# Reordering the steps of a fused attention and token-mixing kernel behind batch 0's first half

## Chip, cores and metric

The kernel runs on one core of a Trainium2 chip. The metric is device time in microseconds (us) of one execution; three runs of the kernel before gave 104.17, 104.23 and 104.53, median 104.23.

## What is computed

Per batch (8 of them) there are 8 heads of 576 rows with 64 columns, and 32 packed queries `p`. Two attentions follow each other, then a token-mixing layer whose weights depend on the data:

```python
p_packed = sm_attn(p, k, v)               # softmax(scale * p k^T) v, per head
out = sm_attn(q, p_packed, p_packed)      # softmax(scale * q p_packed^T) p_packed
x = out.transpose(0, 2, 1, 3).reshape(B, S, H * D)
wq, wk = x @ w_q, x @ w_k                 # 512 -> 64
W_tok = scale * einsum('bsd,btd->bst', wq, wk)
mixed = einsum('bst,btd->bsd', W_tok, x)
return maximum(mixed, 0) @ w_out          # 512 -> 512
```

All inputs and the output are float32; the matmuls run on bfloat16, since the loads convert on the way.

## The kernel before

The program is one written order of small steps, the string `ORDER`. A step reads `NAME.batch.part=banks@engine`: `banks` are the PSUM banks that it writes, `@V`, `@A`, `@P`, `@S` is VectorE (DVE), ScalarE (ACT), GpSimd (POOL) or SyncE (SP), and steps without a letter run on TensorE (PE), but for `LD` (loads, issued by GpSimd) and `ST`, `STF`, `STH`, `HOLD` (issued by SyncE). Each engine executes its own steps strictly in the order of the string, and waits by semaphore for the data and the buffers that a step needs. So the order decides which engine waits where. Eight PSUM banks, three to six buffers of each tile, and four buffers each for k, q and v tie the batches together.

For each batch the steps are, with the engine that does them:

- `LD.k`, `LD.v`, `LD.q`: loads; a `v` is two issues. `KT`, `QV` (DVE, line 237): transpose k and q in 32x32 blocks.
- `S1` (PE, 282), `X1` (ACT, 293), `TE` (DVE, 237): scores of the packed queries, exp, transposition. `PV` (PE, 315), `RC`, `PP` (DVE, 319 and 323): their values and division; `PP` multiplies by the tile `mask`. `PT` (DVE): transposition of the result.
- `QK` (PE, 336), `QKE` (copy out of PSUM), `QD` (POOL, 130): the packed values times `w_k` and `w_q`.
- `S2` (PE, 373), `X2` (ACT, 378), `RS`, `RR` (DVE, 394 and 399): scores of the second attention, exp, sum, reciprocal. `AM` (line 405, POOL or DVE) multiplies the exponentials by the reciprocals; `HA` is a first half of one sum on POOL.
- `AT` (PE, 414 and 419), `AE` (copy): transposition of the attention. `WKQ` (PE, 441 and 446), `WE` (copy), `GM` (PE, 467), `GE` (copy), `Y` (PE, 477), `YE` (copy with scale), `MX`, `MR` (PE, 492 and 498), `RL`, `RLF`, `RLR` (relu): the token mixing without ever forming `out`.
- `OT`, `OH` (PE, 540 and 580): four matmuls with `w_out` per 128 rows; `OE`, `OEF`, `OEH` copy them to the output tile, and the stores follow. The parts of `S2`, `X2`, `RS`, `RR`, `AM`, `AT`, `AE` are ranges of 128-row blocks: 0 is two blocks, 1 the next two, 2 the fifth, 3 all first four, 4 all five.
- `WARM.n` (PE, 619): n filling products of 128 columns on zeros, whose result nobody reads.
- `HOLD.v7`: a tiny DMA on SyncE that waits for batch 7's `v`; every store of SyncE stands behind it.

Output tiles come from six buffers, so batches 6 and 7 write into the tiles of batches 0 and 1, whose stores must have landed:

```python
copy(eng, new("o", b, [P, 4, D], fp32, bufs=NO)[:, 2 * tp:2 * tp + 2], T["ot", b, tp])   # NO = 6
```

In the order, batch b's first attention runs while batch b-1's second attention and batch b-2's output are done, so that TensorE always has independent steps to take.

Of the kernel before, what the change touches and what calls it, by code (L numbers as in the profile page):

```python
# [13 lines left out]
LD.N0@A LD.N1@S SET.warm@V SET.v0@V SET.aT0@V SET.aT1@V SET.aT2@V SET.idf@V LD.W0@A LD.W1@S SET.tab@A LD.h0
LD.g0 LD.v0 LD.r0 LD.q0 LD.k1 NC.0@V PX.0@V NC.1@A PX.1@V SET.aff@P SET.idb@V SET.v3@P KT.0.0@V SET.mask@P
WC.1@P WC.0@P LD.k2 SET.v1@P LD.v1 SET.v2@P KT.0.1@V WARM.4=0 WARM.22.128=0 S1.0=0,1,2,3 X1.0.1@A TE.0.1@V
X1.0.0@A TE.0.0@V WARM.8=4 PV.0.0=4,5 PV.0.1 RC.0@V PP.0.0@V PP.0.1@V LD.q1 PT.0@V WARM.6=6 QK.0=6 QKE.0@A
QV.0.0@V QV.0.1@V QD.0@P WARM.4=7 S2.0.2=2,3 X2.0.2@A RS.0.2@V RR.0.2@V S2.0.0=0,1 LD.v2 S2.0.1=4,5 X2.0.0@A
# [5 lines left out]
RS.1.2@V RR.1.2@V S2.1.1=2,3 X2.1.0@A RS.1.0@V RR.1.0@V WARM.1=6 PV.2.0=6,7 PV.2.1 X2.1.1@A RS.1.1@V RC.2@V
LD.v3 QD.1@P AM.1.2@P AT.1.2=4 RR.1.1@V AM.1.0@P WARM.5=5 AT.1.0=5 AM.1.1@P LD.k4 PP.2.0@V AE.1.2@A PP.2.1@V
PT.2@V QK.2=4 AE.1.0@A QKE.2@A QD.2@P QV.2.2@V LD.q3 LD.v4 AT.1.1=0 AE.1.1@A WKQ.1.0=2,3 WKQ.1.2 WKQ.1.1
WE.1.0@V S2.2.2=6,7 WE.1.1@A X2.2.2@A S2.2.3=4,5 X2.2.3@A GM.1=1 OT.0.0=2,3 GE.1@V Y.1=6,7 OT.0.1 YE.1@A
RS.2.4@V OE.0.0@A MR.1=0,1 MX.1.1=4,5 RLR.1@A RR.2.4@V OT.0.2=6,7 LD.q4 OT.0.3 KT.3.2@V AM.2.3@P OE.0.1@V
RL.1.1@A S1.3=2,3,0,1 X1.3.0@A AM.2.2@P OT.1.4=4 TE.3.0@V LD.k5 AT.2.2=5 X1.3.1@A TE.3.1@V AT.2.3=2 AE.2.3@V
LD.v5 MX.1.0=6,7 AE.2.2@V PV.3.0=0,1 PV.3.1 OEF.1.4@A WKQ.2.0=2,3 WKQ.2.1 RC.3@V PP.3.1@V RL.1.0@A WKQ.2.2  # L30
WE.2.2@A OT.1.2=4,5 OT.1.3 PP.3.0@V PT.3@V QK.3=6 OE.1.1@A LD.q5 KT.4.2@V S1.4=0,1,2,3 GM.2=7 OT.1.0=4,5
X1.4.1@A LD.k6 GE.2@A QKE.3@V X1.4.0@A QV.3.2@V TE.4.1@V Y.2=2,3 YE.2@A S2.3.2=6,7 X2.3.2@A S2.3.3=0,1
X2.3.3@A MX.2.0=2,3 TE.4.0@V RL.2.0@A MR.2=6,7 RLR.2@V OT.1.1 MX.2.1=6,7 RL.2.1@A OE.1.0@A PV.4.0=0,1 QD.3@P
PV.4.1 RS.3.4@V RR.3.4@V LD.v6 AM.3.3@P AM.3.2@P RC.4@V OT.2.0=2,3 OT.2.1 LD.q6 OE.2.0@A PP.4.0@V PP.4.1@V
PT.4@V QK.4=6 AT.3.3=7 QV.4.2@V AT.3.2=0 AE.3.2@A LD.k7 S2.4.2=4,5 AE.3.3@V X2.4.2@A S2.4.3=2,3 X2.4.3@A
KT.5.2@V WKQ.3.0=0,1 WKQ.3.1 WKQ.3.2 RS.4.4@V RR.4.4@V QKE.4@A WE.3.2@A S1.5=4,5,2,3 X1.5.1@A LD.v7 TE.5.1@V
OT.2.2=6,7 AM.4.3@P QD.4@P AM.4.2@P GM.3=0 X1.5.0@A TE.5.0@V GE.3@A OT.2.3 Y.3=2,3 YE.3@V PV.5.0=4,5 PV.5.1
HOLD.v7 MR.3=0,1 RC.5@V PP.5.1@V OE.2.1@A MX.3.0=2,3 PP.5.0@V PT.5@V MX.3.1=6,7 RLR.3@A RL.3.0@A OT.3.4=0
RL.3.1@A AT.4.2=1 AE.4.2@A OEF.3.4@A QV.5.2@V AT.4.3=5 AE.4.3@V ST.1.4@P QK.5=4 QKE.5@V QD.5@P S2.5.2=2,3
X2.5.2@A KT.6.2@V S2.5.3=6,7 X2.5.3@A HA.5@P WKQ.4.0=0,1 WKQ.4.2 LD.q7 WKQ.4.1 WE.4.2@A OT.3.0=2,3  # L40
S1.6=4,5,6,7 X1.6.0@A GM.4=0 GE.4@V TE.6.0@V LD.r7 OT.3.1 X1.6.1@A TE.6.1@V Y.4=0,1 OE.3.0@A RS.5.4@V RR.5.4@V
PV.6.0=4,5 YE.4@A PV.6.1 MX.4.0=6,7 RC.6@V RL.4.0@A PP.6.0@V AM.5.3@P PP.6.1@V PT.6@V MX.4.1=2,3 AM.5.2@P
OT.3.2=0,1 OT.3.3 RL.4.1@A QK.6=4 QKE.6@A QV.6.2@V ST.2.1 S2.6.2=6,7 X2.6.2@A S2.6.3=2,3 ST.3.4 MR.4=4,5
X2.6.3@A OE.3.1@V RLR.4@V KT.7.2@V AT.5.2=6 AE.5.2@A AT.5.3=7 OT.4.0=0,1 OT.4.1 AE.5.3@A WKQ.5.0=4,5 WKQ.5.2
OE.4.0@A ST.0.8@P WKQ.5.1 RS.6.4@V WE.5.2@A RR.6.4@V ST.3.0 ST.4.0 ST.1.8@P S1.7=2,3,6,7 X1.7.1@A AM.6.3@V
OT.4.2=0,1 GM.5=4 TE.7.1@V OT.4.3 AT.6.3=5 X1.7.0@A TE.7.0@V GE.5@A OE.4.1@A AM.6.2@P AT.6.2=4 ST.2.0 Y.5=6,7
YE.5@A ST.3.1 PV.7.0=2,3 QV.7.1@V AE.6.3@V QV.7.0@V AE.6.2@A QD.6@P PV.7.1 RC.7@V PP.7.0@V PP.7.1@V PT.7@V
MR.5=0,1 RLR.5@A MX.5.1=6,7 RL.5.1@A MX.5.0=4,5 RL.5.0@V WKQ.6.0=0,1 WKQ.6.1 WKQ.6.2 WE.6.2@A OT.5.4=2
OEF.5.4@A S2.7.1=6,7 ST.5.4 GM.6=3 GE.6@V X2.7.1@A RS.7.1@V RR.7.1@V S2.7.2=0,1 X2.7.2@A S2.7.0=4,5 QK.7=2
X2.7.0@A RS.7.0@V RR.7.0@V Y.6=6,7 YE.6@A OT.5.2=0,1 MX.6.1=4,5 QKE.7@A MX.6.0=6,7 AM.7.1@P RS.7.2@V RR.7.2@V  # L50
MR.6=2,3 OT.5.3 RLR.6@V RL.6.0@V RL.6.1@A OE.5.1@A ST.4.1 AM.7.0@P OT.5.0=2,3 AM.7.2@P AT.7.0=4 AE.7.0@A
AT.7.1=5 AE.7.1@V AT.7.2=6 AE.7.2@V OT.6.2=0,1 OEF.6.2@A QD.7@P WKQ.7.0=4,5 WKQ.7.2 WKQ.7.1 WE.7.0@A WE.7.1@A
STF.6.2 OT.6.0=6,7 OT.6.1 GM.7=0 OE.6.0@V OT.5.1 OE.5.0@V ST.5.1 GE.7@A Y.7=4,5 OT.6.3 OEF.6.3@V ST.6.0
# [599 lines left out]
```

## Time and profile before

| | |
|---|---|
| median of 3 runs | 104.23 us |
| span of the profiled execution, first to last instruction | 102.8 us |
| around the span, against the median | 1.4 us |
| busy: PE, DVE, ACT, POOL | 92.7, 73.7, 65.0, 51.8 us |
| granted TensorE clock | full in every slice |
| moved by DMA | 25.13 MB, mean 244 GB/s |
| read from and written to HBM | 30.15 and 9.44 MB |
| chain that ended last: PE, DMA, DVE, POOL, ACT | 49%, 21%, 8%, 7%, 6% |

The page gives no time of its own for the profiled execution besides the span, so the difference to the median is taken as what lies around it. Loads keep the DMA engines full at about 210 GB/s until about 72 us; from about 77 to 90 us they move some 410 GB/s, mostly stores. Busy times of PE are modelled, and neighbouring matmuls overlap, so PE is read by the starts of its steps and by where it is idle.

### The profile page before, as it was taken

Reading aid. Unit: us, or ns where it says so; the run is one execution under the profiler, and the core shown is the slowest. Engines: PE = TensorE matmul, PEld = TensorE weight load, DVE = VectorE, ACT = ScalarE, POOL = GpSimd, SP = SyncE. Lnnn points to the kernel's source line nnn. Section 1 sums busy time; section 2 is a strip of 40 time slices with the busy share of each in tenths; the row PEclk is TensorE's granted clock in tenths of the full one; section 3 lists DMA queues with packets and bytes.
Section 4 is the critical chain, followed back from the end, with each engine's and each line's share of the span. In section 5 each row is a group of like instructions: output and inputs, shape, how many; then the busy total and the mean of one; then the engine's idle time right before and its main releaser. Section 6 shows DMA issues by size and latency. Waiting matters only on the chain.

```text
span 102.8 us, 3593 instructions
## 1 busy us (share of the span) xinstructions
PE 92.7 (90%) x1536; PEld 54.6 (53%) x1536; DVE 73.7 (72%) x140; ACT 65.0 (63%) x111; POOL 51.8 (50%) x81
## 2 busy tenths in 40 slices
...
GB/s 9 249 230 207 213 210 213 207 209 213 205 211 207 212 211 210 213 205 212 211 212 207 211 213 204 217 211 203 255 262 409 411 410 408 418 345 264 335 364 160
DMA packets 13279, 25.13 MB, mean 244 GB/s; under 512 B 1040, under 2 KB 6416, under 8 KB 13008
## 3 DMA queue, kind: packets, MB, share of 16 engines
...
q8 instruction: 12, 0.20, 0.7%
...
HBM read 30.15 MB, written 9.44 MB: 385 GB/s over the span
## 4 chain that ended last, share of the span: by engine, by line
PE 49%; DMA 21%; DVE 8%; POOL 7%; ACT 6%; issue 3%; SPq 1%; DVEq 0%; POOLq 0%; ACTq 0%
PE ps L540 26%; DMA q_sb<-in_q_dram 13%; DMA o<-in_moe_w_q_dram 8%; PE ps L373 4%; POOL a L405 4%; PE ps L315 3%; ACT e1T L293 3%; PE ps L419 3%; PE ps L446 3%; DVE rs L394 2%; PE ps L441 2%; PE ps L467 2%; PE ps L282 2%; ACT e L378 1%; DVE qT L237 1%
## 5 line engine op out<-in xcount | busy, mean ns | idle before, releaser
L540 PE MATMUL ps<-wout,relu 128*128 128x512 bf16 x124 | 30.6, 380 | 0.0
L405 POOL TENSOR_TENSOR a<-e,rr 128x256 bf16<-128x256 f32 (+2 forms) x18 | 19.5, 1099 | 17.9 <-DVE rr L399 7.0
L619 PE MATMUL ps<-o 128*128 128x128 f32 (+3 forms) x76 | 19.5, 401 | 1.2 <-DVE o L135 1.2
L540 PEld LDWEIGHTS <-relu 128*128 128x128 bf16 x124 | 10.7, 98 | 11.7 <-issue 1.1
L128 ACT ACTIVATE o<-ps 128x1024 f32<-128x1024 f32 (+2 forms) x13 | 11.3, 871 | 5.4 <-PE ps L540 5.2
L619 PEld LDWEIGHTS ps<-o 128*128 128x128 f32 x76 | 11.3, 209 | 5.2 <-issue 3.6
L503 ACT ACTIVATE relu<-ps 128x1024 bf16<-128x1024 f32 (+1 forms) x14 | 13.0, 968 | 1.1 <-PE ps L492 1.1
L293 ACT ACTIVATE e1T<-ps 128x576 bf16<-128x576 f32 x16 | 9.8, 656 | 5.8 <-PE ps L282 5.2
L378 ACT ACTIVATE e<-ps 128x256 f32<-128x256 f32 (+2 forms) x19 | 11.2, 623 | 2.7 <-PE ps L373 2.5
L394 DVE TENSOR_REDUCE rs<-e 128x16 f32<-128x512 f32 (+2 forms) x13 | 10.9, 840 | 2.3 <-ACT e L378 2.2
L237 DVE STREAM_TRANSPOSE kT<-k_sb 128x1152 uint32<-128x1152 uint32 (+1 forms) x9 | 11.1, 1230 | 1.9 <-DMA k_sb<-in_k_dram 1.9
L173 POOL DMA_DIRECT2D v_sb<-in_v_dram x16 | 10.0, 628 | 4.0 <-DMA v_sb<-in_v_dram 1.6
L237 DVE STREAM_TRANSPOSE qT<-q_sb 128x1152 uint32<-128x1152 uint32 (+1 forms) x10 | 11.0, 1108 | 0.1
L132 DVE COPY o<-ps 128x1024 f32<-128x1024 f32 (+2 forms) x7 | 6.8, 977 | 5.3 <-PE ps L540 2.7
L237 DVE STREAM_TRANSPOSE e<-e1T 128x288 uint32<-128x288 uint32 x16 | 7.4, 468 | 3.1 <-ACT e1T L293 2.7
L128 ACT ACTIVATE aT<-ps 128x128 bf16<-128x128 f32 (+2 forms) x11 | 5.0, 465 | 5.7 <-PE ps L419 3.3
L128 ACT ACTIVATE wkq<-ps 128x448 bf16<-128x448 f32 (+1 forms) x10 | 7.2, 730 | 1.8 <-PE ps L446 1.7
L315 PE MATMUL ps<-v_sb,e 64*64 64x192 bf16 x288 | 7.5, 245 | 0.8 <-DVE e L237 0.5
L315 PEld LDWEIGHTS <-e 64*64 64x64 bf16 x288 | 5.9, 107 | 2.6 <-DVE e L237 2.1
L373 PEld LDWEIGHTS <-qT 64*128 64x128 bf16 x320 | 5.4, 94 | 2.8 <-DVE qT L237 1.7
L373 PE MATMUL ps<-ppT,qT 64*128 64x64 bf16 x320 | 6.6, 190 | 0.2 <-DVE qT L237 0.2
L446 PE MATMUL ps<-aT,pqk 128*128 128x256 bf16 (+1 forms) x48 | 6.8, 246 | 0.0
...
## 6 DMA issues: line engine op xcount, KB each, us to landing
...
out_dram<-o POOLq DMA_DIRECT2D x2, 1024.0 KB, 11.3
...
```

The lines of the kernel that those rows point to most:

```text
L128: nc.scalar.activation(o, i, COPY)
L173: nc.gpsimd.dma_start(v_bufs[b % NL][halves(i), 0:7:2], src)
L237: nc.vector.transpose(o, i)
L293: nc.scalar.activation(e1T[:, x], T["s1", b][x].rearrange("a c m -> a m c"), EXP, scale=scale)
L315: nc.tensor.matmul(T["pv", b][halves(cc), i], lhsT, rhs, start=n == 0, stop=n == R - 1, skip_group_check=True)
L373: nc.tensor.matmul(ps[:, y, t - t0, i], lhsT, rhs, start=e == 0, stop=e == 1)
L378: nc.scalar.activation(e2[:, t0:t1].rearrange("a t (i y n) -> a y (t i) n", i=2, y=2), T["s2", b, c].rearrange("a y t i n -> a y (t i) n") ...
L394: nc.vector.tensor_reduce(rs[:, t0 * H:t1 * H], src, axis=AX, op=ADD)
L405: e.tensor_tensor(a2[:, t0:t1].rearrange("a t i (u l) -> a (t i u) l", l=L), e2v(b, c), T["rr", b][:, t0 * H:t1 * H].to_broadcast((P, (t1 ...
L503: nc.scalar.activation(o, i, RELU)
L540: nc.tensor.matmul(ps, lhsT, wout[:, j, :], start=j == 0, stop=j == NJ - 1)
L619: nc.tensor.matmul(bank(int(bk), [w]), warm[:, 0:P], rhs, start=True, stop=True)
```

## The change

The string `ORDER` is written anew from the first step behind `WKQ.0.1` on; ahead of it the steps are the same and only PSUM banks differ. No step is removed. 34 steps run on another engine, nearly all copies and relus between ScalarE and VectorE; `AM.6.3` goes from VectorE to GpSimd, so that all of line 405 is on GpSimd. Two `WARM.3` are added (six units of filling). The functions are the same; the string is two lines shorter, so a line number after it is smaller by 2.

```diff
-KT.1.2@V AM.0.1@P WARM.3=2 AT.0.1=7 AE.0.1@A AE.0.0@V WKQ.0.0=2,3 WKQ.0.2 WE.0.0@A LD.q2 WKQ.0.1 KT.2.2@V
-S1.1=0,1,4,5 WE.0.1@A GM.0=6 X1.1.0@A TE.1.0@V GE.0@A WARM.2=7 Y.0=2,3 YE.0@V S1.2=0,1,6,7 MR.0=2,3 X1.1.1@A
...
+AT.0.1=1 AE.0.1@A AE.0.0@V WKQ.0.0=6,7 WKQ.0.2 WE.0.0@A LD.q2 WKQ.0.1 WE.0.1@A S1.1=2,3,4,5 KT.2.2@V X1.1.0@A
+GM.0=0 GE.0@V WARM.3=1 LD.O X1.1.1@A S1.2=6,7,2,3 Y.0=0,1 TE.1.0@V X1.2.0@A YE.0@A TE.1.1@V PV.1.0=4,5 MR.0=6,7
...
```

Three places show what moves. The first is VectorE in batch 1, from the last PP.1 to the first reciprocals. `e` out of `e1T` is TE, `qT_268` is QV.1.2, `rs` is RS, `rr` is RR, `rem` is RLR.0. Before:

```order
L237 STREAM_TRANSPOSE e_0_196<-e1T_194 128x9x32 x2
L319 RECIPROCAL rec_240<-ps 128x2
L323 SCALAR_TENSOR_TENSOR pp_244<-ps,rec_240,mask 128x128 x2
L237 STREAM_TRANSPOSE ppT_250<-pp_244 128x128
L237 STREAM_TRANSPOSE qT_268<-q_sb_74 128x2x2x288
L132 CAST pqk_264<-ps 128x2x128
L394 TENSOR_REDUCE rs_283<-e_1_84 128x8
L399 RECIPROCAL rr_286<-rs_283 128x8
L394 TENSOR_REDUCE rs_283<-e_1_84 128x16
```

and now:

```order
L317 RECIPROCAL rec_240<-ps 128x2
L321 SCALAR_TENSOR_TENSOR pp_244<-ps,rec_240,mask 128x128 x2
L235 STREAM_TRANSPOSE ppT_250<-pp_244 128x128
L235 STREAM_TRANSPOSE qT_268<-q_sb_74 128x2x2x288
L235 STREAM_TRANSPOSE e_0_196<-e1T_194 128x9x32 x2
L503 TENSOR_SCALAR rem_561<-ps 128x4x64
L392 TENSOR_REDUCE rs_283<-e_1_84 128x16 x2
L397 RECIPROCAL rr_286<-rs_283 128x16 x2
L392 TENSOR_REDUCE rs_283<-e_1_84 128x8
```

TE.2 has moved from ahead of RC.1 to behind QV.1.2, RLR.0 has come to VectorE, QKE.1 has left it, and the small sum now comes last.

The second place is ScalarE a little later, from batch 1's AE to batch 0's output. `aT1` is AE.1, `e2_0` is X2.2, `wkq_1` is WE.1, `o_0` is OE.0. Before:

```order
L128 ACTIVATE aT1_81<-ps_61 128x2x64
L128 ACTIVATE aT1_81<-ps_61 128x2x256
L128 ACTIVATE pqk_2_265<-ps_61 128x2x128
L128 ACTIVATE aT1_81<-ps_61 128x2x256
L128 ACTIVATE wkq_1_364<-ps_61 128x448
L378 ACTIVATE e2_0_83<-ps_61 128x2x2x64
L378 ACTIVATE e2_0_83<-ps_61 128x2x8x64
L484 ACTIVATE y_1_430<-ps_61 128x256
L128 ACTIVATE o_0_85<-ps_61 128x1024
```

and now:

```order
L126 ACTIVATE aT1_81<-ps_61 128x2x256
L501 ACTIVATE relu_0_528<-ps_61 128x1024
L126 ACTIVATE aT1_81<-ps_61 128x2x256
L376 ACTIVATE e2_0_83<-ps_61 128x2x2x64
L376 ACTIVATE e2_0_83<-ps_61 128x2x8x64
L126 ACTIVATE aT1_81<-ps_61 128x2x64
L126 ACTIVATE wkq_1_364<-ps_61 128x448 x2
L126 ACTIVATE o_0_85<-ps_61 128x1024
```

The small AE.1.2 was first and now comes behind X2.2; both WE.1 stand behind it; RL.0.0 has moved between the two large AE.1. On TensorE the steps there read `S2.2.2 S2.2.3 WKQ.1.0 OT.0.2 AT.1.2 WKQ.1.2 OT.0.3 GM.1 OT.0.0 S1.3`, where before they read `WKQ.1.0 WKQ.1.2 WKQ.1.1 S2.2.2 S2.2.3 GM.1 OT.0.0 Y.1 OT.0.1 MR.1 MX.1.1 OT.0.2 OT.0.3 S1.3`. On GpSimd, LD.k3 and LD.v3 have moved from ahead of QD.1 to behind it, LD.v3 between AM.1.0 and AM.1.2.

The third place is the end of GpSimd's queue. `a` is AM, `pqk` is QD, `out_dram<-o_85` and `o_86` are ST.0.8 and ST.1.8. Before:

```order
L405 TENSOR_TENSOR a_2_330<-e_1_84,rr_286 128x256
L561 DMA out_dram<-o_85 64x2x2048
L561 DMA out_dram<-o_86 64x2x2048
L405 TENSOR_TENSOR a_0_328<-e_0_83,rr_285 128x256
L130 COPY pqk_263<-pqk_263 128x2x64
L405 TENSOR_TENSOR a_1_329<-e_1_84,rr_286 128x512 x2
L405 TENSOR_TENSOR a_1_329<-e_1_84,rr_286 128x256
L130 COPY pqk_264<-pqk_264 128x2x64
```

and now:

```order
L403 TENSOR_TENSOR a_0_328<-e_0_83,rr_285 128x1024
L403 TENSOR_TENSOR a_0_328<-e_0_83,rr_285 128x256
L128 COPY pqk_263<-pqk_263 128x2x64
L403 TENSOR_TENSOR a_1_329<-e_1_84,rr_286 128x256
L559 DMA out_dram<-o_85 64x2x2048
L403 TENSOR_TENSOR a_1_329<-e_1_84,rr_286 128x512 x2
L128 COPY pqk_264<-pqk_264 128x2x64
L559 DMA out_dram<-o_86 64x2x2048
```

AM.6.3 (128x1024) has joined AM.6.2 here, and the two stores have moved from ahead of batch 6's products to batch 7's, one of them to the very end.

More of the change, by code (lines that the diff above doesn't have):

```diff
@@ L13 @@
 ORDER = """
[L14 to L18, printed above, removed]
@@ L19 @@
-RS.0.0@V RR.0.0@V X2.0.1@A RS.0.1@V RR.0.1@V AM.0.2@P WARM.6=7 AT.0.2=7 AE.0.2@A AM.0.0@P WARM.5=6 AT.0.0=6
-KT.1.2@V AM.0.1@P WARM.3=2 AT.0.1=7 AE.0.1@A AE.0.0@V WKQ.0.0=2,3 WKQ.0.2 WE.0.0@A LD.q2 WKQ.0.1 KT.2.2@V
-S1.1=0,1,4,5 WE.0.1@A GM.0=6 X1.1.0@A TE.1.0@V GE.0@A WARM.2=7 Y.0=2,3 YE.0@V S1.2=0,1,6,7 MR.0=2,3 X1.1.1@A
-TE.1.1@V MX.0.0=4,5 X1.2.0@A LD.O PV.1.0=0,1 TE.2.0@V PV.1.1 X1.2.1@A TE.2.1@V RC.1@V LD.k3 PP.1.0@V PP.1.1@V
-PT.1@V MX.0.1=6,7 QV.1.2@V RLR.0@A QK.1=2 QKE.1@V RL.0.0@A WARM.3=3 S2.1.2=4,5 S2.1.0=0,1 RL.0.1@A X2.1.2@A
@@ L24 @@
[L24 to L53, printed above, removed]
@@ L54 @@
-STF.6.3 YE.7@A ST.5.0 MR.7=6,7 RLR.7@A MX.7.0=4,5 RLF.7.0.1@A RLF.7.0.0@V MX.7.1=2,3 RLF.7.1.0@A OT.7.4=0
-OEF.7.4@A ST.7.4 RLF.7.1.1@V OT.7.1=6 OEF.7.1@V OT.7.0=7 STF.7.1 OT.7.2=1 OEF.7.0@A OH.7.0=0 STF.7.0 OEF.7.2@A
-STF.7.2 OEH.7.0@V STH.7.0 OH.7.1=5 OEH.7.1@A STH.7.1@A
+LD.N0@A LD.N1@S SET.warm@V SET.v0@V SET.aT0@V SET.aT1@V SET.aT2@V SET.idf@V LD.W0@A LD.W1@S SET.tab@A LD.h0 LD.g0
+LD.v0 LD.r0 LD.q0 LD.k1 NC.0@V PX.0@V NC.1@A PX.1@V SET.aff@P SET.idb@V SET.v3@P KT.0.0@V SET.mask@P WC.1@P WC.0@P
@@ new lines @@
+LD.k2 SET.v1@P LD.v1 SET.v2@P KT.0.1@V WARM.4=0 WARM.22.128=0 S1.0=0,1,2,3 X1.0.1@A TE.0.1@V X1.0.0@A TE.0.0@V
+WARM.8=4 PV.0.0=4,5 PV.0.1 RC.0@V PP.0.0@V PP.0.1@V LD.q1 PT.0@V WARM.6=6 QK.0=0 QKE.0@A QV.0.0@V QV.0.1@V QD.0@P
+WARM.4=6 S2.0.2=6,7 X2.0.2@A RS.0.2@V RR.0.2@V S2.0.0=2,3 LD.v2 S2.0.1=4,5 X2.0.0@A RS.0.0@V RR.0.0@V X2.0.1@A
+RS.0.1@V RR.0.1@V AM.0.2@P WARM.6=1 AT.0.2=0 AE.0.2@A AM.0.0@P WARM.5=1 AT.0.0=0 KT.1.2@V AM.0.1@P WARM.3=1
+AT.0.1=1 AE.0.1@A AE.0.0@V WKQ.0.0=6,7 WKQ.0.2 WE.0.0@A LD.q2 WKQ.0.1 WE.0.1@A S1.1=2,3,4,5 KT.2.2@V X1.1.0@A
@@ new lines @@
+GM.0=0 GE.0@V WARM.3=1 LD.O X1.1.1@A S1.2=6,7,2,3 Y.0=0,1 TE.1.0@V X1.2.0@A YE.0@A TE.1.1@V PV.1.0=4,5 MR.0=6,7
+PV.1.1 RC.1@V X1.2.1@A PP.1.0@V PP.1.1@V WARM.3=0 MX.0.1=0,1 PT.1@V QV.1.2@V WARM.2=2 QK.1=2 WARM.3=3 RL.0.1@A
+S2.1.2=4,5 TE.2.1@V QKE.1@A X2.1.2@A S2.1.1=0,1 TE.2.0@V X2.1.1@A QD.1@P RLR.0@V WARM.1=3 S2.1.0=2,3 PV.2.0=4,5
+X2.1.0@A RS.1.1@V RS.1.0@V RR.1.1@V RR.1.0@V RS.1.2@V LD.k3 PV.2.1 WARM.5=6 RC.2@V AM.1.1@P AT.1.1=0 PP.2.1@V
+AE.1.1@A AM.1.0@P RR.1.2@V PP.2.0@V MX.0.0=6,7 LD.v3 PT.2@V QK.2=1 RL.0.0@A WKQ.1.1=2,3 AM.1.2@P QV.2.2@V AT.1.0=0
@@ new lines @@
+S2.2.2=4,5 S2.2.3=6,7 AE.1.0@A WKQ.1.0 X2.2.2@A OT.0.2=4,5 AT.1.2=0 X2.2.3@A QKE.2@V RS.2.4@V LD.k4 AE.1.2@A
+WKQ.1.2 WE.1.0@A WE.1.1@A OT.0.3 GM.1=0 RR.2.4@V OE.0.1@A KT.3.2@V OT.0.0=6,7 LD.q3 S1.3=2,3,4,5 GE.1@A Y.1=0,1
+X1.3.1@A AM.2.3@P X1.3.0@A QD.2@P OT.0.1 YE.1@V AT.2.3=0 AM.2.2@P AT.2.2=1 OE.0.0@A LD.v4 LD.q4 TE.3.1@V TE.3.0@V
+AE.2.3@V MX.1.1=4,5 PV.3.0=2,3 MX.1.0=6,7 AE.2.2@A LD.k5 PV.3.1 RL.1.1@V RC.3@V LD.v5 WKQ.2.0=0,1 PP.3.0@V WKQ.2.1
+WKQ.2.2 RL.1.0@A MR.1=4,5 KT.4.2@V OT.1.2=6,7 PP.3.1@V WE.2.2@A RLR.1@A GM.2=0 GE.2@V S1.4=4,5,2,3 X1.4.0@A PT.3@V
```

24 lines of the change are left out of this document (added).

## The prediction

> **What bounds the kernel now.** I read the page first, then busy time by stretches, then the chain of waits, then the timelines of VectorE, ScalarE and GpSimd.
>
> ```profile
> span 102.8 us, 3593 instructions
> PE 92.7 (90%) x1536; PEld 54.6 (53%) x1536; DVE 73.7 (72%) x140; ACT 65.0 (63%) x111; POOL 51.8 (50%) x81
> ```
>
> PE is busy for 90% of the span. An average over stages doesn't say where the rest is, so the same numbers by stretch (columns: stretch; its length; busy us of PE, its weight loads, DVE, ACT, POOL; granted clock; DMA share; GB/s):
>
> ```profile
> 28.90:34.97 6.07, 5.43 (x116) 3.82 (x117) 5.18 (x13) 3.11 (x7) 4.54 (x7) 1.00 1.17 210
> 34.97:40.40 5.43, 5.43 (x88) 2.56 (x87) 3.56 (x4) 4.38 (x7) 3.35 (x5) 1.00 1.16 209
> 40.40:55.00 14.60, 13.93 (x272) 7.57 (x273) 12.30 (x22) 11.19 (x17) 8.11 (x12) 1.00 1.14 210
> 55.00:64.00 9.00, 8.63 (x204) 5.59 (x205) 7.64 (x14) 7.84 (x15) 6.37 (x9) 1.00 1.15 210
> 64.00:82.00 18.00, 17.48 (x364) 10.71 (x357) 16.27 (x29) 15.61 (x26) 8.43 (x10) 1.00 1.11 277
> 82.00:99.00 17.00, 16.92 (x177) 8.73 (x175) 10.61 (x19) 11.06 (x21) 2.86 (x4) 1.00 0.92 365
> ```
>
> From 34.97 on PE is idle for 0.00 + 0.67 + 0.37 + 0.52 + 0.08 = 1.64 us in 64. The clock is full throughout. So the end of PE is its work plus those 1.64 us, and an order of steps can win little more than that. Until 64 the DMA engines are full at 210 GB/s, that is, loads land at a rate that no order on the engines changes. Rows of the chain of waits (start, us, what) tell where that sets the time, and what the tail is:
>
> ```profile
> 13.89 13.59 DMA q_sb<-in_q_dram
> 27.51 1.39 DVE qT L237
> ...
> 98.09 0.67 PE ps L580 x4
> ...
> 98.85 0.56 DVE o L132
> ```
>
> Batch 1's q lands at 27.48, and its transposition (QV.1.2) runs to 28.90. LD.q1 and all loads queued ahead of it keep their places in the change, so 28.90 is a fixed point for both kernels. At the other end PE's chain finishes at 98.76, and 4.0 us of copy and store follow. The median of the runs, 104.23, is 1.4 us more than the span.
>
> **Up to the fixed point.** Six more units of filling matmuls and GE.0, YE.0, MX.0.0 in other places all lie ahead of 28.90 or inside time in which PE would wait, for q1 above all. I cost them at nothing; without that cover the two new WARM.3 would be 1.8 us, by this row of one of them:
>
> ```profile
> 27.85 0.91 PE L619 MATMUL ps<-o 128*128 128x384 f32 x2
> ```
>
> **28.90 to 34.97: VectorE gets later.** In the kernel before, both TE.2 have been done ahead of QV.1.2; now they and RLR.0 stand behind it.
>
> ```profile
> 25.27 1.02 DVE L237 STREAM_TRANSPOSE e<-e1T 128x288 uint32<-128x288 uint32 x2 [0.34 <-ACT e1T L293]
> 30.27 0.63 DVE L394 TENSOR_REDUCE rs<-e 128x16 f32<-128x512 f32 x1
> 30.94 0.25 DVE L399 RECIPROCAL rr<-rs 128x16 f32<-128x16 f32 x1
> 32.73 1.34 DVE L237 STREAM_TRANSPOSE qT<-q_sb 128x1152 uint32<-128x1152 uint32 x1
> L323 DVE SCALAR_TENSOR_TENSOR pp<-ps,rec,mask 128x128 bf16<-128x128 f32 x16 | 4.8, 340 | 0.3
> L505 DVE TENSOR_SCALAR rem<-ps 128x256 bf16<-128x256 f32 x3 | 1.2, 415 | 0.6 <-PE ps L498 0.6
> L405 POOL TENSOR_TENSOR a<-e,rr 128x512 bf16<-128x512 f32 x6 | 6.2, 1049 | 6.8 <-ACT y L484 6.4 <-DVE rr L399 0.4
> ```
>
> 28.90 + 1.02 + 0.41 = 30.3; two sums of 0.63 and two reciprocals of 0.25, slightly overlapped, end at 31.95; the third sum, RC.2, two PP.2 of 0.34 with a reciprocal between and PT.2 take about 1.65 more, to 33.6 (an estimate from these rows); QV.2.2 ends at 33.6 + 1.34 = 34.9, not 34.07. AM.1.1 on GpSimd starts at 31.9 and AM.1.1, AM.1.0 end at 34.0 (2 x 1.05). LD.v3 (two issues of 0.63) now stands ahead of AM.1.2, which therefore starts near 35.3. Before, all three had ended at 33.39.
>
> ```profile
> 22.91 0.63 POOL L173 DMA_DIRECT2D v_sb<-in_v_dram  x1
> 31.34 2.05 POOL L405 TENSOR_TENSOR a<-e,rr 128x512 bf16<-128x512 f32 x2 [0.22 <-DVE rr L399]
> 34.97 0.78 PE L373 MATMUL ps<-ppT,qT 64*128 64x64 bf16 x40
> ```
>
> S2.2 starts at 34.97 before, because PE was then busy with WKQ.1; now it starts there because QV.2.2 ends at 34.9. LD.v3 goes out 11 us later (34.0 for 22.91), and LD.k3 behind QD.1, but q2, the output weights and k3 itself are queued ahead, so I cost this at nothing on the DMA side (bounds 0 and 1.3 us, the two issues of LD.v3). So both kernels stand at S2.2 at 34.97, and PE has this left that was done before: WKQ.1.0, WKQ.1.2 and AT.1.2. Their prices, and those of a change of matmul shape, from the chain of waits:
>
> ```profile
> 62.87 0.06 PE ps L414 x2
> ...
> 75.38 0.12 PE ps L441 x4
> 75.50 0.22 PE ps L446 x2
> 75.72 0.06 PE ps L441 x2
> 75.78 0.06 PE ps L446 x2
> ...
> 76.17 0.41 PE ps L282 x20
> 76.58 0.97 PE ps L540 x4
> 77.55 0.29 PE ps L467 x10
> 77.84 0.86 PE ps L540 x4
> ```
>
> Extra work: 0.34 + 0.12 + 0.06 = **+0.52**. The four matmuls of an OT take 0.97 behind an S1 (32-row shape) and 0.86 behind a GM of their own shape: about 0.1 for each change of shape. Counted in ORDER from S2.2.3 on, 55 pairs of neighbours on PE differ in shape before and 57 now: **+0.2**. The Trainium skill, "TensorEngine Tiling (Array Packing)", Key Properties, says that changing the tiling mode drains TensorE; the trace agrees, with 0.11 here.
>
> **34.97 to 41: new waits.** AT.1.2 stands behind OT.0.2, then AE.1.2 on ScalarE, then WKQ.1.2, with nothing between on PE, and OT.0.3 and GM.1 queued behind:
>
> ```profile
> L128 ACT ACTIVATE aT<-ps 128x128 bf16<-128x128 f32 x6 | 1.7, 282 | 2.2 <-PE ps L414 2.2
> L128 ACT ACTIVATE wkq<-ps 128x448 bf16<-128x448 f32 x5 | 2.6, 544 | 0.8 <-PE ps L446 0.8
> 38.93 1.38 DVE L237 STREAM_TRANSPOSE kT<-k_sb 128x1152 uint32<-128x1152 uint32 x1
> ```
>
> The end of AT, 0.28 on ScalarE and two semaphores of about 0.05 leave PE idle for 0.5. GM.1 then waits for the second of two WE.1 (0.54 each, only OT.0.3 between): 0.2. S1.3 waits for KT.3.2 (end 40.3, as before, since X2.2.3, RS.2.4 and RR.2.4 keep their times): 0.3. Sum 1.0; before, this stretch had none. At 40.7 OT.0.1, Y.1, MR.1 and MX.1.1 are still to do, about 1.4 us of PE.
>
> **41 to the end.** I carried the steps on by the same rows. In favour: OT.1.4 now fills the place where PE waited for AM.3.3 (that is most of the 0.67 us up to 55), QK.4 no longer stands ahead of it. Against: RR.4.4 now stands behind both TE.5, RS.5.4 still waits for HA.5, and TE.6.1 stands behind RR.5.4, so PV.6 waits as before. I find PE waits of 0.9 in this part, against 1.64. Sum of waits after 34.97: 1.0 + 0.9 = 1.9, **+0.3**; bounds 0.0 (-1.6) and twice what I found (+2.2).
>
> The products themselves: AM.6.3 goes from VectorE to GpSimd.
>
> ```profile
> 61.77 0.60 POOL L405 TENSOR_TENSOR a<-e,rr 128x256 bf16<-128x256 f32 x1
> 76.67 1.23 DVE L405 TENSOR_TENSOR a<-e,rr 128x1024 bf16<-128x1024 f32 x1
> 76.79 1.58 POOL L405 TENSOR_TENSOR a<-e,rr 128x256 bf16<-128x256 f32 x1 [3.22 <-DVE rr L399]
> ```
>
> GpSimd's small product took 1.58 beside VectorE's, and 0.60 alone: 0.98 was lost. Now both run on GpSimd, one behind the other. The chain's rows above stay on PE without a break from 75.38 to 78.70, so nobody waited for that 0.98: I take 0 on the path, with bounds -0.98 and +1.1 (1024 elements on GpSimd are 2.05 by the pair at 31.34, so the small one would end near 79.5 and not at 78.37). The Trainium skill, "SBUF — State Buffer" (the reading of its diagram), says that the two engines share a port pair under an exclusive lock, and the loser blocks for the whole instruction: the trace agrees, since 0.98 is most of the 1.23.
>
> **Sum.** PE's end 98.76 + 0.52 + 0.2 + 0.3 = 99.8; the tail has the same length (the last copy of 384 columns on VectorE, one store behind it), so the span is 103.8 and the time, with the 1.4 around it, **105.3** (1.0 over the median).
>
> **Rivals.** (1) *PE fed without a gap.* If the waits behind S2.2 all vanish, the time is 104.23 - 1.64 + 0.72 = 103.3. For it: work on PE is nearly unchanged, and OT steps are placed between dependent steps. Against: AT.1.2 to WKQ.1.2 has nothing between. It decides if PE waits less than 0.4 us behind 34.97. Chance 0.10. (2) *Keeping the products apart pays.* If GpSimd's 0.98 was on a path after all (AM.6.2, AT.6.2, WKQ.6), and nothing new comes, the time is 104.23 - 0.98 = 103.25. Against: PE didn't wait there. The lock of the skill's page would be its mechanism. Chance 0.03. (3) *The late start is made good*: waits of 0.9 in all, so that the 0.72 of work is paid for by them: 104.2. Chance 0.20. (4) *Stores hold buffers.* ST.0.8 and ST.1.8 (1 MB each) go out behind AM.7.2 and QD.7, at about 86 and 89, instead of 72 and 73.
>
> ```profile
> out_dram<-o POOLq DMA_DIRECT2D x2, 1024.0 KB, 11.3
> 72.28 1.29 POOL L561 DMA_DIRECT2D out_dram<-o  x2
> ```
>
> Batch 6's output tile is batch 0's: by the steps carried on, OE.6.0 on ScalarE wants it at 93.3, and RLF.7.0.0 is queued behind. If the store lands 11.3 us after its issue as before, it is 97.3: +4.0, 109.3; with 9.3, 107.3. It decides from 7.3 us. Against: in the row, loads were ahead of it in the queue, and at 86 none are. Chance 0.15.
>
> **How the numbers follow.** The forecast, chance 0.52, runs from 104.8 to 106.0 on its own. A measurement tells about 0.5% from no change. Faster: (1) and (2), 0.13. Within: (3), 0.20. Slower: forecast and (4), 0.67. The range leaves out about half of the faster cases and the upper part of (4): 103.5 to 107.3.
>
> **What would show it.** Right: S2.2 on PE near 35.0; WKQ.1.2 near 37.5 behind a gap of 0.5; S1.3 near 40.3 with OT.0.1 behind it; PE's chain ending near 99.8. Wrong: S2.2 more than 0.5 off, PE idle after it for less than 1 us or more than 3, a pause in the loads between 35 and 46 (LD.v3, LD.v4 late), or OE.6.0 waiting for a DMA.

## The result, and the profile after

The changed kernel takes 106.11 us (median of 4 runs, 105.37 to 106.27) beside 104.37 for the kernel before on the same chip: ratio 1.0141, 95% interval 1.0097 to 1.0185. It is slower, by about 1.7 us, and 0.8 above the predicted 105.3. The profiled execution took 105.98 with a span of 104.2. Each run lists its span beside its time, and the two differ by 1.7 to 1.8, not by the 1.4 that the prediction took from a median and the span of another run. Here and below, ratios and intervals leave out executions that fell in a slower state, while medians are over all.

First the page's totals, and busy time by the stretches that the prediction used (stretch; length; busy PE, weight loads, DVE, ACT, POOL; granted clock; DMA share; GB/s):

```profile
span 104.2 us, 3577 instructions
PE 93.9 (90%) x1522; PEld 56.3 (54%) x1540; DVE 71.7 (69%) x142; ACT 64.7 (62%) x108; POOL 52.8 (51%) x82
34.97:40.40 5.43, 4.77 (x103) 2.81 (x97) 3.13 (x3) 4.17 (x8) 3.71 (x5) 1.00 1.13 183
82.00:99.00 17.00, 16.79 (x176) 8.81 (x177) 11.47 (x21) 10.44 (x19) 4.15 (x6) 1.00 1.00 395
```

Three things differ from before. PE, idle for 0.00 us between 34.97 and 40.40 before, is idle there for 0.66. The DMA engines move 183 GB/s in that stretch instead of 209. And from 82 to 99 their share is 1.00 where it was 0.92, at 395 GB/s for 365. The trace lacks 18 of 1540 matmul records, so PE's idle time further down is read from a sister kernel below, whose records are whole.

The last row of PE in the chain of waits, and SyncE's last issue:

```profile
98.44 0.66 PE ps L578 x4
99.71 0.54 SPq L588 DMA_DIRECT2D out_dram<-o  x1
```

PE's chain ends at 99.10, 0.34 later than before (98.76) and not 1.0 later. But the span is 1.4 longer. The missing 1.1 us lies behind PE. (The 0.34 itself goes with a late load in this execution, batch 3's q; its row is shown further down.) The last two stores are the only one of 192 KB on SyncE (issued at 99.71, before at 99.44) and the only one of 64 KB on ScalarE (99.65, before 99.31). Their DMA rows (size; us from issue to landing) in the kernel before:

```profile
out_dram<-o SPq DMA_DIRECT2D x1, 192.0 KB, 2.5
out_dram<-o ACTq DMA_DIRECT2D x1, 64.0 KB, 2.0
```

and in the changed one:

```profile
out_dram<-o SPq DMA_DIRECT2D x1, 192.0 KB, 3.3
out_dram<-o ACTq DMA_DIRECT2D x1, 64.0 KB, 3.6
```

Before, the later of the two landed at 99.44 + 2.5 = 101.9; now it is 99.65 + 3.6 = 103.25. The stores are issued 0.3 later, as PE's end is, and take 1.0 longer. Why they land late shows in the DMA columns of 2-us stretches, here of the kernel before:

```profile
76.00:78.00 2.00, 2.00 (x50) 1.08 (x49) 1.93 (x4) 2.00 (x4) 1.21 (x1) 1.00 1.10 356
92.00:94.00 2.00, 2.00 (x18) 0.70 (x17) 2.00 (x3) 0.51 (x2) 0.00 (x0) 1.00 0.60 231
94.00:96.00 2.00, 1.95 (x12) 0.77 (x10) 1.81 (x3) 1.82 (x4) 0.00 (x0) 1.00 0.77 304
```

and of the changed one:

```profile
76.00:78.00 2.00, 1.95 (x48) 1.08 (x49) 1.91 (x4) 1.57 (x4) 0.42 (x1) 1.00 1.01 236
92.00:94.00 2.00, 2.00 (x22) 0.98 (x22) 0.55 (x2) 1.69 (x4) 0.00 (x0) 1.00 1.01 420
94.00:96.00 2.00, 2.00 (x12) 0.93 (x11) 2.00 (x4) 1.08 (x3) 0.00 (x0) 1.00 0.96 365
102.00:103.00 1.00, 0.00 (x0) 0.00 (x0) 0.00 (x0) 0.00 (x0) 0.00 (x0) 1.00 0.09 31
```

Before, 356 GB/s moved when the loads ran out (76 to 78), and from 92 to 96 the engines had time to spare (shares of 0.60 and 0.77): they had caught up with the stores issued so far, and little was left ahead of the last one. After, 236 GB/s moved in 76 to 78, the share stayed at 0.96 or more from 82 to 100, and packets still ran behind 102 (before, none did). Counted from the start, the DMA engines had moved 14.8 MB by 72 us before and 14.5 after (205 and 202 GB/s), and 16.4 and 15.9 MB by 78 (281 and 229 GB/s in between). So the changed kernel was 0.5 MB behind at 78, or 1.3 us at 400 GB/s (an estimate from these rates). What was missing at 76 to 78 are ST.0.8 and ST.1.8, 1 MB each. On GpSimd they go out here (start, us, operation):

```profile
77.58 2.49 POOL L403 TENSOR_TENSOR a<-e,rr 128x1024 bf16<-128x1024 f32 x2 [4.71 <-DVE rr L397]
85.23 0.67 POOL L559 DMA_DIRECT2D out_dram<-o  x1
88.17 0.68 POOL L559 DMA_DIRECT2D out_dram<-o  x1
```

at 85.23 and 88.17, where it was 72.28 and 72.9. That is the theory to test: **late stores leave the transfers nothing to move when the loads end, and the backlog stands ahead of the last store.** Rivals: the late loads (LD.k3, LD.v3), the late start of batch 1 on VectorE, SyncE's new order of stores, the added fillers, and the product AM.6.3 on GpSimd.

### The profile page after: what moved, and what is told of

Read it like the earlier page. It is cut to its first block, busy times and chain, and to the rows that moved or that the text cites. A ratio compares the mean times of both kernels' runs of the same rounds, so it can differ in the third digit from the quotient of the medians.

```text
span 104.2 us, 3577 instructions
## 1 busy us (share of the span) xinstructions
PE 93.9 (90%) x1522; PEld 56.3 (54%) x1540; DVE 71.7 (69%) x142; ACT 64.7 (62%) x108; POOL 52.8 (51%) x82
## 4 chain that ended last, share of the span: by engine, by line
PE 70%; ACT 7%; DMA 7%; DVE 5%; issue 4%; POOL 2%; DVEq 0%; ACTq 0%; POOLq 0%
PE ps L538 25%; PE ps L617 11%; DMA k_sb<-in_k_dram 7%; PE ps L313 6%; PE ps L371 4%; PE ps L417 4%; PE ps L280 4%; PE ps L490 3%; PE ps L444 3%; PE ps L439 3%; PE ps L465 3%; ACT e L376 2%; DVE rs L392 2%; PE ps L334 2%; DVE kT L235 2%
## 5 line engine op out<-in xcount | busy, mean ns | idle before, releaser
L538 PE MATMUL ps<-wout,relu 128*128 128x512 bf16 x109 | 28.6, 380 | 1.3 <-issue 0.8
L403 POOL TENSOR_TENSOR a<-e,rr 128x256 bf16<-128x256 f32 (+2 forms) x19 | 20.5, 1093 | 15.5 <-DVE rr L397 14.3
L617 PE MATMUL ps<-o 128*128 128x128 f32 (+3 forms) x80 | 21.8, 416 | 1.2 <-DVE o L133 1.2
L126 ACT ACTIVATE o<-ps 128x1024 f32<-128x1024 f32 (+2 forms) x15 | 13.7, 923 | 3.9 <-PE ps L538 3.6
L617 PEld LDWEIGHTS ps<-o 128*128 128x128 f32 x80 | 12.4, 215 | 5.8 <-issue 3.9
L126 ACT ACTIVATE aT<-ps 128x128 bf16<-128x128 f32 (+1 forms) x9 | 3.8, 422 | 6.9 <-PE ps L417 5.1
L126 ACT ACTIVATE wkq<-ps 128x448 bf16<-128x448 f32 (+1 forms) x9 | 6.3, 707 | 0.9 <-PE ps L444 0.5
L439 PE MATMUL ps<-pqk,aT 128*128 128x64 bf16 x80 | 6.0, 194 | 0.7 <-ACT aT L126 0.6
```

The costliest lines, as they stand in the source:

```text
L126: nc.scalar.activation(o, i, COPY)
L403: e.tensor_tensor(a2[:, t0:t1].rearrange("a t i (u l) -> a (t i u) l", l=L), e2v(b, c), T["rr", b][:, t0 * H:t1 * H].to_broadcast((P, (t1 ...
L538: nc.tensor.matmul(ps, lhsT, wout[:, j, :], start=j == 0, stop=j == NJ - 1)
L617: nc.tensor.matmul(bank(int(bk), [w]), warm[:, 0:P], rhs, start=True, stop=True)
```

## The experiments

Diffs show the written order, one step to a line. Each median stands beside that of the kernel before in the same set of runs (104.41 for e1 to e4, 104.40 for e5 to e8, 104.46 for the last four).

**e1: the two loads put back** to about where they stood.

```diff
 LD.O
+LD.k3
+LD.v3
...
-LD.k3
...
-LD.v3
```

> The changed order, with LD.k3 and LD.v3 back where they were (behind LD.O, ahead of QD.1 and AM.1). The changed kernel is at 106.1 us, the one before at 104.4. Theory T (tail): the stores reach the DMA engines late, and the last one lands 3.2 us behind its issue, not 2.1; PE itself is only 0.3 late. Theory L (loads): the pause of the loads between 35 and 44 us, about 0.2 MB or 1 us, shifts all that follows. Theory P (PE order): the time is lost where VectorE, ScalarE and PE wait for each other in batch 1. L expects 105.1 (1.0 less). T expects 105.6: loads end 1 us earlier, which frees 0.2 MB or 0.5 us at 400 GB/s for stores. P expects 106.1.

Measured 105.53, ratio 1.0105 (1.0085 to 1.0126). About 0.4 us comes back by the ratios (0.6 by the medians), but the interval overlaps that of the changed kernel (1.0097 to 1.0185), so a gain isn't shown. The value is the one that T expected (105.6); L's 105.1 is ruled out.

**e2: the two stores put back.**

```diff
 LD.r7
+ST.0.8@P
+ST.1.8@P
...
-ST.0.8@P
...
-ST.1.8@P
```

> The changed order, with ST.0.8 and ST.1.8 back behind the last load on GpSimd's queue (issued near 73 us, not 85 and 88). T expects 105.1 (the 2 MB then go out while SyncE's stores wait for their copies, and the last store lands 2.1 us after its issue). L and P expect 106.1.

Measured 104.72, ratio 1.0033 (1.0003 to 1.0062): two steps moved give back 1.4 of the 1.7 us by the medians (1.1 of 1.5 by the ratios). Its 192 KB store lands 2.3 us after issue, the 64 KB store 2.5, and the engines have slack again:

```profile
out_dram<-o SPq DMA_DIRECT2D x1, 192.0 KB, 2.3
94.00:96.00 2.00, 2.00 (x11) 0.91 (x10) 2.00 (x5) 0.62 (x2) 0.00 (x0) 1.00 0.67 256
```

**e3: TE.2 put back ahead of RC.1** (here X1.2.1 also stands ahead of TE.1.1, and since both use the one buffer of `e1T`, TE.1.1 waits for X1.2.1 and reads batch 2's values).

```diff
 YE.0@A
+X1.2.1@A
 TE.1.1@V
...
+TE.2.0@V
+TE.2.1@V
 RC.1@V
-X1.2.1@A
...
-TE.2.1@V
...
-TE.2.0@V
```

> The changed order, with X1.2.1, TE.2.0 and TE.2.1 ahead of RC.1, as before, so that VectorE does them while it waits for batch 1's q. AM.1 should start 0.9 us earlier. P expects 105.3 (0.8 less). T and L expect 106.1 or 0.2 less.

Measured 106.96 and 107.10, ratio 1.0251 (1.0219 to 1.0283). It puts a wait of its own in (VectorE is idle for 1.98 us ahead of TE.1.1) and says nothing on TE.2; e8 has the move in a form that isolates it.

**e4: the two added fillers taken out.**

```diff
-WARM.3=1
...
-WARM.3=0
```

> The changed order without the two added WARM.3 (those behind GM.0 and ahead of MX.0.1; it computes the same). If they are covered by the wait for batch 1's q, 106.1. If they are on the path, 104.3 (1.8 less). If they keep the TensorE clock up, more than 106.1, with a granted clock below 1 in the early slices.

Measured 105.77, ratio 1.014 (1.0097 to 1.0183), as the changed kernel. No cost of the fillers shows; the interval leaves room for some 0.4 us.

**e5: SyncE's stores in the order of before**, GpSimd's two stores left late.

```diff
 ST.2.1
+ST.3.4
+ST.3.0
+ST.4.0
+ST.2.0
+ST.3.1
 X2.7.2@A
...
 OEF.5.4@V
+ST.5.4
 ST.4.1
```

(the same steps are taken out further down).

> The changed order, with SyncE's stores in the order before (2.1, 3.4, 3.0, 4.0, 2.0, 3.1, 5.4, 4.1, then as changed), so that ST.4.1, which waits for its copy to 79.7 us, holds no finished store back; ST.0.8 and ST.1.8 stay late on GpSimd's queue. Theory T (the DMA engines get their stores too late, between 77 and 82 us by the trace, and then never catch up): 105.4, 0.5 to 0.9 under the changed kernel's 106.1. If only the lateness of the two 1 MB stores counts: 106.1.

Measured 106.34, ratio 1.0181 (1.0155 to 1.0207): nothing comes back, where theory T in this form expected 105.4. It is not SyncE's order.

**e6: the kernel before, with AM.6.3 on GpSimd.**

```diff
-AM.6.3@V
+AM.6.3@P
```

> The kernel before with one edit: AM.6.3 on GpSimd and not on VectorE, so that no product of line 405 runs on VectorE. That the blocked product cost 0.98 us on the path: 103.5. That it cost nothing, since PE had no wait there (the prediction's reading): 104.4, 0 to 0.3 more, as AM.6.2 then ends about 1.1 us later.

Measured 104.83, ratio 1.0039 (1.0025 to 1.0053). In the old order the move doesn't pay, it costs 0.4 us. The profile shows where. PE in the kernel before, with OT.4.3, AT.6.3 behind it, and PV.7:

```profile
77.67 1.03 PE L540 MATMUL ps<-wout,relu 128*128 128x512 bf16 x4
79.22 0.91 PE L315 MATMUL ps<-v_sb,e 64*64 64x192 bf16 x36
```

and GpSimd and PE in e6 (in brackets idle time and what ended it):

```profile
76.52 2.48 POOL L402 TENSOR_TENSOR a<-e,rr 128x1024 bf16<-128x1024 f32 x2 [3.25 <-PE ps L279]
77.38 1.03 PE L537 MATMUL ps<-wout,relu 128*128 128x512 bf16 x4
78.48 0.45 PEld L416 LDWEIGHTS <-a 128*128 128x128 bf16 x8 [0.57 <-POOL a L402]
79.30 0.91 PE L312 MATMUL ps<-v_sb,e 64*64 64x192 bf16 x36
```

At OT.4.3 e6 was 0.29 ahead of the kernel before, at PV.7 it was 0.08 behind: 0.37 us went between them, where the weights of AT.6.3 wait for the large product on GpSimd. That product ended at 77.90 on VectorE and ends at about 78.4 on GpSimd. In the chain of before, from which the prediction read 0 on the path, nobody waits for this product, and still 0.5 us more of it make AT.6.3 wait.

**e7: e1 and e2 together.**

> The changed order with both repairs: LD.k3, LD.v3 early and ST.0.8, ST.1.8 behind the last load. If T and L are the whole loss: 104.2 or less (the stores' repair alone gave 104.7, the loads' alone 105.5, of 106.1). If the early loads act only through the tail: as with the stores alone, 104.7.

Measured 104.80, ratio 1.0034 (1.0022 to 1.0047): as e2 alone. So no cost of the late loads shows once the stores go out early (e2's interval is 0.6 us wide); in e1 they acted, if at all, through the same backlog.

**e8: e7, with TE.2 put back** (X1.2.1 behind TE.1.1).

```diff
 TE.1.1@V
+X1.2.1@A
...
+TE.2.0@V
+TE.2.1@V
 RC.1@V
-X1.2.1@A
...
-TE.2.1@V
...
-TE.2.0@V
```

> As the kernel with both repairs, and TE.2.0, TE.2.1 with X1.2.1 ahead of RC.1 but behind TE.1.1 (in the earlier try X1.2.1 stood ahead of TE.1.1, which then waited for it and read batch 2's values). Theory P, that VectorE's lateness in batch 1 costs: 0.5 to 0.8 less than with both repairs alone, 103.6. If the time to 40 us is set by loads and the end by stores: the same as with both repairs.

Measured 104.73, ratio 1.0020 (1.0002 to 1.0037), no different from e7: VectorE's late start in batch 1 costs nothing that shows at the end.

**e9: e7, with AM.6.3 back on VectorE.**

```diff
-AM.6.3@P
+AM.6.3@V
```

> The changed order with LD.k3, LD.v3 behind LD.O, with ST.0.8, ST.1.8 behind LD.r7, and with AM.6.3 back on VectorE, beside AM.6.2 on GpSimd. Theory (the product's move to GpSimd is the last 0.3 to 0.4 us, as it was 0.4 in the kernel before): 104.4, ratio 1.000, AM.6.2 again about 1.6 us long. Rival (products apart is worth keeping, the blocked 0.98 us of GpSimd counts): 105 or more. Rival (the rest is the order of TensorE's steps, the product's move nothing): 104.8 as with the two repairs alone.

Measured 105.70, ratio 1.0122 (1.0092 to 1.0152): 0.9 us slower than e7. The first two theories differed over the sign, and the rival was right on it: in the new order the move of the product is worth 0.9. But it isn't GpSimd's blocked time. VectorE and PE in e9 (start, us, operation, in brackets idle time and what ended it):

```profile
77.15 0.61 POOL L402 TENSOR_TENSOR a<-e,rr 128x256 bf16<-128x256 f32 x1 [3.46 <-DVE rr L396]
77.33 1.51 DVE L402 TENSOR_TENSOR a<-e,rr 128x1024 bf16<-128x1024 f32 x1
78.76 0.47 DVE L234 STREAM_TRANSPOSE e<-e1T 128x288 uint32<-128x288 uint32 x1
79.28 0.94 PE L312 MATMUL ps<-v_sb,e 64*64 64x192 bf16 x36 [1.02 <-DVE e L234]
99.11 0.66 PE ps L577 x4
```

and in e7:

```profile
76.62 1.01 DVE L234 STREAM_TRANSPOSE e<-e1T 128x288 uint32<-128x288 uint32 x2
77.87 0.94 PE L312 MATMUL ps<-v_sb,e 64*64 64x192 bf16 x36
```

In e9 the product stands on VectorE ahead of TE.7.0, PE waits 1.02 us for that transposition before PV.7.0, and its chain ends at 99.77. In e7 both transpositions run back to back, PE doesn't wait, and its chain ends at 98.36 in an execution that was 0.3 ahead of e9 from S2.2 on. GpSimd's own product took 0.61, unblocked; this time VectorE's was the one that was slowed, 1.51 for 1.23. The Trainium skill, "SBUF — State Buffer", Who interferes with whom, says that the order of issue decides which of the two blocks; these rows agree as to who lost time (GpSimd began at 77.15, VectorE at 77.33 and lost 0.28), as do those of before, where VectorE began first and GpSimd lost 0.98.

**e10: only ST.0.8 put back.**

```diff
 LD.r7
+ST.0.8@P
...
-ST.0.8@P
```

> The changed order with ST.0.8 alone moved to behind LD.r7; ST.1.8 stays at the end of GpSimd's queue. Theory A (what counts is that the transfers have nothing to move when the loads run out: 236 GB/s in 76 to 78): one store of 1 MB, 2.5 us at 400 GB/s, fills the hole, so most of the 1.4 us comes back: 105.0, and the stretch from 76 to 78 moves over 300 GB/s. Theory B (each late megabyte counts by itself, since the last stores stand behind it): half comes back: 105.4. Rival (buffers of batch 1's tile, only ST.1.8 counts): no change, 106.1.

Measured 104.67, ratio 1.0033 (1.0013 to 1.0052), the same as with both. ST.1.8 still goes out at 87.62, and that is harmless:

```profile
76.00:78.00 2.00, 2.00 (x50) 0.99 (x18) 1.90 (x5) 1.68 (x3) 0.73 (x1) 1.00 1.12 305
94.00:96.00 2.00, 2.00 (x11) 0.89 (x10) 2.00 (x5) 0.73 (x2) 0.00 (x0) 1.00 0.73 278
out_dram<-o SPq DMA_DIRECT2D x1, 192.0 KB, 2.2
```

One store under way when the loads run out is enough: theory A's 105.0 is nearer than B's 105.4, and A's 300 GB/s are there. So a late megabyte doesn't count by itself; what fits is the time that the engines lose about 76 to 78. That one window doesn't price the loss, though: e1 moved only 183 GB/s in it, and its span is 103.7; it had moved more up to 72 us (205 GB/s for the changed kernel's 202).

**e11: the kernel before, with the two stores late.**

```diff
-ST.0.8@P
...
-ST.1.8@P
...
 QD.6@P
+ST.0.8@P
...
 QD.7@P
+ST.1.8@P
```

> The kernel before with ST.0.8 behind QD.6 (about 78.6 instead of 72.3) and ST.1.8 behind QD.7 (about 87.8 instead of 72.9); all else as before. Theory (late big stores make the transfers run to the end without slack): the 1.6 us of slack that the kernel before has between 90 and 96 takes up part of it, the rest of some 1.4 shows at the end: 104.8 to 105.5, the last packet 0.4 to 1.1 later than at 101.56. Rival (lateness of these stores costs nothing by itself, only together with the changed order): 104.4. Rival (buffers: OEF.6.2 wants batch 0's tile at 89.0, OEF.7.4 batch 1's at 95.5): a wait for a DMA at one of these and 106 or more.

Measured 105.28, ratio 1.0082 (1.0058 to 1.0105). The old order with late stores has the same symptoms:

```profile
76.00:78.00 2.00, 2.00 (x34) 1.08 (x19) 1.90 (x4) 1.99 (x4) 1.73 (x2) 1.00 0.66 162
94.00:96.00 2.00, 2.00 (x10) 0.91 (x11) 1.35 (x4) 1.47 (x3) 0.00 (x0) 1.00 0.98 378
97.57 0.66 PE ps L577 x4
out_dram<-o SPq DMA_DIRECT2D x1, 192.0 KB, 3.5
```

162 GB/s where 356 moved, no slack from 94 to 96, and a last store of 3.5 us (the 64 KB store took 3.2). This execution ran about 0.5 ahead of that of before from 28 us on, so PE's chain ended 0.5 earlier (98.23), and yet the span is 103.4, 0.6 longer. No copy waited for a buffer: OEF.6.2 and OEF.7.4 came 0.5 earlier than before too. So the backlog alone, without any of the rest of the change, makes the kernel slower, and by what was expected (104.8 to 105.5).

**e12: loads, stores, TE.2, AM.6.3 and the fillers all put back.**

> The changed order with the loads, the two stores, TE.2 and AM.6.3 put back and without the two added WARM.3: what is left of the change is the order of TensorE's steps and the copies between ScalarE and VectorE. Theory (the parts named make the whole loss): 104.2 to 104.5, ratio 0.998 to 1.001. Rival (TensorE's order costs 0.3 or more, as the prediction had it): 104.8 or more, PE's chain ending at 99.0 or later.

Measured 105.25, ratio 1.0081 (1.0052 to 1.0109). The theory failed here for the reason that e9 shows: with AM.6.3 on VectorE, PE's chain ends at 99.60 and is idle for 1.05 us between 78 and 80.

```profile
78.00:80.00 2.00, 0.95 (x45) 0.90 (x46) 1.90 (x4) 1.11 (x2) 0.00 (x0) 1.00 1.02 413
98.93 0.67 PE ps L577 x4
```

No version beat the kernel before. Those with an early store (e2, e7, e8, e10) stay at ratios of 1.0020 to 1.0034. Their spans tell the same: the medians over the executions are 102.8 to 103.0, and 102.6 and 102.7 for the kernel before in the same sets (its profiled 102.8 is on the long side). What that last 0.2 to 0.35 us is, these runs do not tell.

## Why the prediction was right

It was right in sign and within its range, and that is in good part luck: 106.11 lies just above the stretch that the forecast itself covered (104.8 to 106.0), and what made the time wasn't what it counted. By its own sum the span was 99.8 + 4.0; measured it was 99.1 + 5.1, and 1.8 around it instead of 1.4. PE came out 0.7 too late in the sum, the tail 1.1 too short. Without the late stores the same order takes 104.7 (e2, e10). Two of its own signs of being wrong came true, too: PE's idle time behind S2.2 is below 1 us (0.89 in e10), and the loads pause.

**Up to S2.2: right.** AM.1.1, LD.v3 and AM.1.2 came where they were put (31.9, 34.0 and 35.3); QV.2.2 ended at 34.55, 0.35 earlier than the 34.9 of the sum, and S2.2 began at 34.75, not 34.97:

```profile
33.21 1.34 DVE L235 STREAM_TRANSPOSE qT<-q_sb 128x1152 uint32<-128x1152 uint32 x1
31.91 2.06 POOL L403 TENSOR_TENSOR a<-e,rr 128x512 bf16<-128x512 f32 x2 [2.33 <-DVE rr L397]
33.91 1.29 POOL L171 DMA_DIRECT2D v_sb<-in_v_dram  x2
35.21 0.64 POOL L403 TENSOR_TENSOR a<-e,rr 128x256 bf16<-128x256 f32 x1
34.75 0.91 PE L371 MATMUL ps<-ppT,qT 64*128 64x64 bf16 x40
```

**The new waits, 34.97 to 41: right in place, two thirds in size.**

```profile
37.39 0.23 PE L439 MATMUL ps<-pqk,aT 128*128 128x64 bf16 x2 [0.37 <-ACT aT L126]
40.10 0.47 PE L280 MATMUL ps<-kT,pT 32*32 32x288 bf16 x32 [0.21 <-DVE kT L235]
```

WKQ.1.2 begins at 37.39 behind a gap of 0.37 (0.5 predicted), S1.3 at 40.10 behind 0.21 (0.3); GM.1 has no gap (0.2). In all PE is idle there for 0.66, where 1.0 was predicted.

**The extra work of 0.72: somewhat too small.** e10 has every matmul record. Its PE is idle behind 34.97 for 0.61 + 0.14 + 0.08 + 0.03 + 0.03 = 0.89 us, 0.75 less than before, and its chain ends at the same 98.76. Its S2.2 began at 34.73, 0.24 earlier than before, so from S2.2 on PE's work grew by about 0.75 + 0.24 = 1.0 us.

```profile
34.97:40.40 5.43, 4.82 (x102) 2.82 (x97) 3.13 (x3) 4.15 (x8) 3.70 (x5) 1.00 1.11 187
40.40:55.00 14.60, 14.46 (x267) 8.02 (x243) 11.63 (x21) 11.70 (x18) 9.88 (x15) 1.00 1.13 210
55.00:64.00 9.00, 8.92 (x199) 5.55 (x197) 7.90 (x15) 8.06 (x13) 6.02 (x9) 1.00 1.15 209
64.00:82.00 18.00, 17.97 (x370) 10.92 (x371) 14.58 (x29) 16.39 (x26) 9.38 (x11) 1.00 1.11 268
82.00:99.00 17.00, 16.97 (x177) 8.81 (x175) 11.37 (x21) 10.19 (x19) 3.52 (x5) 1.00 0.98 387
```

**Waits from 41 on: wrong.** 0.9 predicted, 0.28 there in e10. The prediction had RS.5.4 wait for HA.5 and TE.6.1 stand behind RR.5.4, and that is so, but "so PV.6 waits as before" is the step that failed. PV.6 in the kernel before, and TE.6.1 with PV.6 in the changed one:

```profile
68.58 0.94 PE L315 MATMUL ps<-v_sb,e 64*64 64x192 bf16 x36 [0.47 <-DVE e L237]
69.31 0.42 DVE L235 STREAM_TRANSPOSE e<-e1T 128x288 uint32<-128x288 uint32 x1
69.93 0.94 PE L313 MATMUL ps<-v_sb,e 64*64 64x192 bf16 x36
```

TE.6.1 ends later than before (69.73 for 68.52), but PE is busy with other steps until PV.6 begins, so the wait of 0.47 is gone; those for AM.3.3 and KT.5.2 are gone as well. The term "AM.6.3 ... 0 on the path" is no reason for this: it was read from the chain of before, and e6 shows 0.37 us of wait there, while in the new order AT.6.3 stands behind PV.7 and the product on VectorE would have cost 1.02 (e9). That e9's PE ends at 99.77, near the predicted 99.8, is chance. Rival 2 has a size near that 1.02, but not its mechanism, and rival 3 (waits make up for the work) is what PE did.

**"The tail has the same length": wrong, 5.1 us for 4.0.** It was taken from the last copy and store by themselves, not from what is queued on the DMA engines ahead of that store. The late stores were seen, but only as holders of buffers (rival 4, decided from 7.3 us of landing time). That rival's condition was nearly met and did not bite: ST.0.8 landed 6.9 us after issue, at 92.1, and OE.6.0 began at 92.59, earlier than the 93.3 I had for it, without a wait. The same two lines of the order cost through another mechanism.

**LD.k3 and LD.v3 "at nothing": not quite.** The pause in the loads that I named as a sign of error is there (183 GB/s in 34.97 to 40.40), and so the reading that no order on the engines changes the rate of the loads does not hold. In the profiled execution a late load also reaches PE, that of batch 3's q:

```profile
47.60 1.38 DVE L235 STREAM_TRANSPOSE qT<-q_sb 128x1152 uint32<-128x1152 uint32 x1 [0.73 <-DMA q_sb<-in_q_dram]
```

S2.3 so begins 14.28 us behind S2.2, and 13.96 in e2, which has no such wait: 0.32, nearly all of the 0.34 by which PE ends later than before. Of five profiles with the late loads (e3 left aside), two have such a wait (after and e10) and three have none (e2, e4, e5); of the four with the early loads (e1, e7, e9, e12) none has. So it differs from one execution to the next, and that the late loads are its cause is argued, not shown. On the time, the late loads are worth 0.0 with the stores early (e7 against e2) and about 0.4, not shown, with them late (e1).
